# Attention with a threshold and a shrinking layer on one core: some k and q turned on TensorE instead of by DMA, v loaded in three pieces, other slots

## The chip, the cores and the metric

The kernel runs on one core of a Trainium2 chip. The metric is the device time in microseconds (us) of one execution. Inputs lie in HBM as 32-bit floats, and the output goes there too. The engines of the core are TensorE (PE, with its weight loads shown apart as PEld), VectorE (DVE), ScalarE (ACT), GpSimd (POOL) and SyncE (SP), which here only issues DMAs.

## The reference

```python
# q, k, v: (8, 8, 576, 64); tau = 0.02
scores = scale * np.matmul(q, k.transpose(0, 1, 3, 2))       # scale = 1/8
thresh = np.max(scores, axis=-1, keepdims=True) - tau
scores = np.where(scores >= thresh, scores, -1e9)
attn = softmax(scores)
x = np.matmul(attn, v)            # -> (8 * 576, 512): heads side by side
h = x @ w_in                      # w_in (512, 2048)
out = (h - np.tanh(h)) @ w_out    # w_out (2048, 512)
```

## The kernel before, in words

**Pairs and tiles.** The 64 heads are taken two at a time, as 32 pairs (p = 0 to 31, four per batch entry). A pair has 9 tiles of 128 score rows: four for each head, and one that both share, since 576 rows are 4.5 x 128. The shared tile is the last one of an even pair and the first one of an odd pair, so two shared tiles stand next to each other, once in 18 tiles (their matmuls are on L387, all others on L396). There are 288 tiles.

**Work for a pair.** k, q and v are loaded. `split` (L222, GpSimd) scales k or q and writes it as a high and a low 16-bit half side by side (khl, qhl). `turn` (L297) transposes these nine 128x128 blocks into kT or qT of 128x1152. `swap` (L318, GpSimd) writes kS, which is kT with its halves exchanged. `split_v` (L255, GpSimd) writes v into one of four buffers vb.

**Work for a tile.** `scores` (L373): matmuls of qT with kT and kS into a PSUM tile psS of the pool ps_big, which has two buffers; VectorE scales it into sc and takes its row maxima (L406). `kink` (L425): ScalarE makes z from sc with the threshold. z is transposed, by TensorE for the first six pairs (L452), later by a DMA that SP issues for two tiles at once (L440, zT). `weights` (L442): ScalarE's exponential gives pT (L469). `attend` (L474): matmuls with vb into psO. `norm` and `emit_x` bring the result to xT.

**The layer.** Once the four pairs of a batch entry are done, `layers` (L630) hands out 16 h steps (four matmuls, L565, then tanh on ScalarE, L578, and a subtraction on VectorE, L584) and 16 y steps (four matmuls, L591). A string PATTERN (L622) says for each of 36 slots which step comes in it. After the last tile the rest of the layer runs alone.

**The order.** There is no scheduler: every engine executes its instructions in the order in which the main loop (L820) issues them. A slot s issues the scores of tile s + 8, kink of tile s + 5, weights of tile s, the layer steps of the slot, attend, and last the steps in `plan[s]`. The tables PREP (for pairs 1 to 7) and LATER (for pairs from DUAL = 8 on, one for even and one for odd pairs, L746) put a pair's loads, splits, turns and swap into the plan. An entry (what, d) means: d slots ahead of the slot that issues the pair's first scores, which is 9p - 8. k0, q0, q1, v0, v1 are loads, ks, qs, vs the splits, kt, qt the turns, and kw the swap.

**Who turns.** For pairs below 8, `turn` uses nine transposing matmuls (L281) into a PSUM tile of ps_big and one VectorE copy (L313), then calls `swap`. From pair 8 on, both k and q go through a transposing DMA that SP issues (L301), and the swap is a plan step of its own. The same SP queue issues the zT transposes and the stores of the output.

**Loads from pair 8 on** are issued by ScalarE (`load_part`, L143). v goes in two DMAs: four of the nine rows of each group to partitions 0 to 63, five to partitions 64 to 127. The pools of raw data, khl and qhl, and kT, qT and kS have two buffers for each name.

Of the kernel before, what the change touches and what calls it, by code (L numbers as in the profile page):

```python
# [9 lines left out]
F32 = mybir.dt.float32  # L10
# [8 lines left out]
def kernel(  # L19
# [12 lines left out]
    P = 128  # L32

    B, H, S, D = q.shape
# [11 lines left out]
    HPAIR = H // 2  # L46
# [5 lines left out]
    TPP = 9  # L52
# [10 lines left out]
    AHEAD = 8  # L63
# [48 lines left out]
    raw_pool = pool("raw", 2)  # L112
# [21 lines left out]
    raws = {}  # L134
    DUAL = 8
    AT_ONCE = 1
    LOADER = nc.scalar

    boths = {}

    def load_part(p, t, part):  # L143


        b, h0 = p // HPAIR, 2 * (p % HPAIR)
        if part == 0:
            both = raw_pool.tile([P, 2, 10, D], F32, name=f"{t}raw", tag=t)
            both = boths[t] = both[:, 0:AT_ONCE, :, :]
            for a in range(AT_ONCE):  # L150
                raws[p + a, t] = both[:, a, :, :]
        both = boths[t]
        rows = {"k": k, "q": q, "v": v}[t][b, h0 : h0 + 2 * AT_ONCE, :, :]
        heads = both.rearrange("p a (h c) d -> p (a h) (c d)", h=2)
        if t == "k":
            dst = both[:, :, 0:TPP, :].rearrange("p a c d -> p a (c d)")
            rows = rows.rearrange("(a h) s d -> a (h s) d", h=2).rearrange(
                "a (p c) d -> p a (c d)", c=TPP
            )
        elif t == "v":  # L160
            rows = rows.rearrange("h (p c) d -> p h (c d)", c=TPP)
            if part == 0:
                dst, rows = heads[0:64, :, 0 : 4 * D], rows[:, :, 0 : 4 * D]
            else:
                dst, rows = heads[64:P, :, :], rows[:, :, 4 * D :]
        elif part == 0:
            dst = heads[:, :, 0 : 4 * D]
            rows = rows[:, 0:512, :].rearrange("h (p c) d -> p h (c d)", c=4)
        else:
            dst = both[:, part - 1, 4, :]  # L170
            rows = rows[2 * part - 2 : 2 * part, 512:S, :].rearrange("h s d -> s h d")
        LOADER.dma_start(out=dst, in_=rows)

    def load(p, t):
        b, h0 = p // HPAIR, 2 * (p % HPAIR)
        hs = slice(h0, h0 + 2)
        src = {"k": k, "q": q, "v": v}[t]
        eng = nc.sync
        r = raw_pool.tile([P, 2, 10, D], F32, name=f"{t}raw", tag=t)[:, 0, :, :]
        raws[p, t] = r  # L180
        eng.dma_start(
            out=r.rearrange("p (h c) d -> p h (c d)", h=2)[:, :, 0 : 4 * D],
            in_=src[b, hs, 0:512, :].rearrange("h (p c) d -> p h (c d)", c=4),
        )
        rem = src[b, hs, 512:S, :].rearrange("h s d -> s h d")
        if t == "v":
            eng.dma_start(out=r[0:64, 4:10:5, :], in_=rem)
        else:
            eng.dma_start(out=r[:, 4, :], in_=rem)

    def load_first(t, h, eng):

        src = {"k": k, "q": q}[t]
        if (0, t) not in raws:
            raws[0, t] = raw_pool.tile([P, 2, 10, D], F32, name=f"{t}raw", tag=t)[:, 0, :, :]
        r = raws[0, t]
        if h is None:
            rem = src[0, 0:2, 512:S, :].rearrange("h s d -> s h d")
            eng.dma_start(out=r[:, 4, :], in_=rem)
        else:  # L200
            eng.dma_start(
                out=r[:, 5 * h : 5 * h + 4, :].rearrange("p c d -> p (c d)"),
                in_=src[0, h, 0:512, :].rearrange("(p c) d -> p (c d)", c=4),
            )
# [17 lines left out]
    def split(p, t):  # L222
        x = raws.pop((p, t))[:, 0:9, :]
        hl = hl_pool.tile([P, TPP, 2, D], FP16, name=f"{t}hl", tag=t)
        nc.gpsimd.tensor_scalar(  # L225
            out=x, in0=x, scalar1=QKSC, scalar2=1.0, op0=ALU.mult, op1=ALU.mult
        )
        nc.gpsimd.tensor_copy(out=hl[:, :, 0, :], in_=x)
        nc.gpsimd.tensor_tensor(  # L229
            out=hl[:, :, 1, :], in0=x, in1=hl[:, :, 0, :], op=ALU.subtract  # L230
        )
        hls[p, t] = hl
# [22 lines left out]
    def split_v(p):  # L255
        r, vb = raws.pop((p, "v")), vbs[p % NV]
        lo = 64 if p >= DUAL else 0
        nc.gpsimd.tensor_copy(
            out=vb[:, :, 0:4, 0:D],
            in_=r.rearrange("p (h c) d -> p h c d", h=2)[:, :, 0:4, :],  # L260
        )
        nc.gpsimd.tensor_copy(out=vb[0:64, :, 4, 0:D], in_=r[lo : lo + 64, 4:10:5, :])
        nc.gpsimd.tensor_copy(out=vb[64:P, :, 5, 0:D], in_=r[lo : lo + 64, 4:10:5, :])
# [13 lines left out]
    def turn_chunk(out, c, lhsT, mixed=True):  # L277
# [4 lines left out]
            out=out, lhsT=lhsT, rhs=rhs, is_transpose=True, start=True, stop=True  # L282
        )

    def k_lead(p):
        if p < HPAIR + 2:
            return 6 if p in (2, 4) or p == HPAIR + 1 else 5 - (p == 1)
        return (6, 6)[1 - p % 2]

    def q_by_dma(p):  # L290

        return p >= DUAL

    def k_by_dma(p):
        return p >= DUAL

    def turn(p, t):  # L297
        hl = hls.pop((p, t))
# [19 lines left out]
    def swap(p):  # L318
        m = mats[p, "k"]
        sw = qk_tile("ks")  # L320
        for lo, hi in ((0, D), (D, 0)):
            o, i = sw[lo : lo + D, 0:W], m[hi : hi + D, 0:W]
            nc.gpsimd.tensor_copy(out=o, in_=i)  # L323
        mats[p, "ks"] = sw
# [264 lines left out]
    def project(m, ms, part, ps, last, cols=slice(0, d_model)):  # L589
# [31 lines left out]

    PATTERN = lambda m: {  # L622
        0: '-h--h-hh--h-hh-h-hh-h--hh-h--hh-y-yy',
        B - 2: 'hyhyhyhyhyhyhyhyhyhyhyhyhyhyhyhy',
    }.get(m, 'h-yhyhhyhyyhyyhh-yhhyhhy-yhyyh-yyhhy')

    FIRST = 3
    quarters = lambda m: [(m, ms, part) for ms in range(4) for part in range(4)]
# [86 lines left out]
    def w_cast():  # L715
        flat, wt, i, cols = loaded.pop(0)
        nc.gpsimd.tensor_copy(out=flat[:, i * cols : (i + 1) * cols], in_=wt)  # L717

    def w_load(piece):
# [6 lines left out]
        else:  # L726
# [18 lines left out]

    LATER = {  # L746
        0: (
            ("k0", 17), ("q0", 15), ("v0", 13), ("kt", 7), ("q1", 15),
            ("ks", 8), ("v1", 12), ("vs", 6), ("qs", 10), ("qt", 7),
            ("kw", 3),  # L750
        ),
        1: (
            ("k0", 19), ("v1", 14), ("q0", 18), ("v0", 16), ("qs", 11),
            ("q1", 17), ("qt", 8), ("ks", 13), ("vs", 6), ("kt", 10),
            ("kw", 7),
        ),
    }
    for p in range(DUAL, NPAIR):
        first = TPP * p - AHEAD
        at = lambda d, f: plan.setdefault(first - d, []).append(f)  # L760
        for what, d in LATER[p % 2]:
            t, w = what
            f = {
                "0": lambda p=p, t=t: load_part(p, t, 0),
                "1": lambda p=p, t=t: load_part(p, t, 1),
                "2": lambda p=p, t=t: load_part(p, t, 2),
                "s": lambda p=p, t=t: split_v(p) if t == "v" else split(p, t),
                "t": lambda p=p, t=t: turn(p, t),
                "w": lambda p=p, t=t: swap(p) if k_by_dma(p) else None,
            }[w]  # L770
            at(d, f)
    for p in range(1, DUAL):
        first = TPP * p - AHEAD
        for d, f in PREP[3 if p == 1 else 0 :]:
            d -= p == 1 and d == 3
            if p > HPAIR and d >= LDK - 2:
                d = ((16, 14, 12), (17, 15, 13))[1 - p % 2][LDK - d]
            elif d in (7, 8) and q_by_dma(p):
                d = ((9, 9) if d == 7 else (10, 10))[1 - p % 2]
            elif d == 4:  # L780
                d = 4
            elif d == 5:
                d = k_lead(p)
            elif p in (2, 4):
                d = {8: 9, 7: 8}.get(d, d)
            plan.setdefault(first - d, []).append(lambda p=p, f=f: f(p))
        d = (6, 7)[1 - p % 2] if q_by_dma(p) else 3 - (p == 1 or p >= 5)
        d = 4 if p in (2, 4) else d
        plan.setdefault(first - d, []).append(lambda p=p: turn(p, "q"))

    load(0, "v")
# [8 lines left out]
        load(1, t)  # L800
    pieces = w_pieces()
    load_when = [3, 8, 13, 18, 21, 25, 29, 34, 38, 42, 46, 49, 52, 55, 58, 61]
    cast_when = [11, 19, 27] + [4 * i + 32 for i in range(3)] + [3 * i + 44 for i in range(10)]

    todo, stage = [], 0
    fold = const.tile([P, 64], BF16, name="fold")
# [3 lines left out]
            plan.setdefault(-AHEAD, []).extend(plan.pop(at))  # L810


    kinks, wts, atts = {}, {}, {}
    for i in range(NTILE + 3):
        at = i - 4 if i < HPAIR * TPP else i
        atts.setdefault(at + LAG, []).append(i)
        if i < NTILE:
            wts.setdefault(at, []).append(i)
            kinks.setdefault(i // 2 * 2 + 2 - AHEAD if i < 4 else i - MASK, []).append(i)
    for s in range(-AHEAD, NTILE + LAG + 3):  # L820
        p, j = divmod(max(s, 0), TPP)
# [43 lines left out]
                emit_x(pp - 1)  # L865
        for step in plan.pop(s, []):
            step()
        if s + AHEAD in cast_when:
            w_cast()
        if s + AHEAD in load_when:  # L870
            w_load(next(pieces))

    for _, step in todo:
# [16 lines left out]
    _ = bass_utils  # L890
# [35 lines left out]
```

## Time and profile before

| what | value |
|---|---|
| three timed runs | 511.3, 513.72, 514.99 us; median 513.72 |
| the profiled execution | 509.47 us, of which the span of the trace is 507.7 |
| TensorE's mean granted clock | 0.995 |
| DMA | 95.61 MB, 234,525 packets, 205,152 of them under 512 B |
| SP's DMA queue | 213,520 packets, 73.17 MB, 74.7% of 16 engines |
| ScalarE's DMA queue | 20,944 packets, 21.67 MB, 15.7% of 16 engines |
| transposing DMAs | zT x117, kT x24, qT x24; median 4.4 to 4.9 us from issue to landing |
| transposing matmul on k or q | 72 each, a record of 220 ns |
| copy of its PSUM tile on VectorE | 757 ns |

The page of the profile first gives each engine's busy time, share of the span and number of instructions; then the span in 40 equal slices, where a digit is the busy share in tenths; then the DMA queues, the chain of work that ended last, and the costliest groups of instructions. In an answer by windows each engine's busy time stands with its number of instructions, and the granted clock, the DMA share and GB/s close the line. A DMA share above 1 comes from packets that overlap. In a timeline a row has start, duration, engine, line, operation and tiles, and in brackets the idle time ahead of it with what ended it. The ends of matmuls are modelled, so their starts are the surer numbers.

### The profile page before, as it was taken

To read this page: it belongs to the slowest core of one execution; us is meant where nothing else is said; L and a number is where in the kernel's file an instruction comes from. 1 tells how busy PE (TensorE), PEld (TensorE's weight loads), DVE (VectorE), ACT (ScalarE), POOL (GpSimd) and SP (SyncE) were. 2 spreads that over 40 slices of the span, in tenths; PEclk is the share of its full clock that TensorE was granted. 3 is DMA by queue.
4 is the path that set the end of the run, shared out by engine and by line. 5 is a ranking of instruction groups with operands and counts; after the bars stand their busy time and mean duration, and the time that the engine had idled before them with its cause. 6 is when DMAs were issued, how large, how long until landed. Compare 5 with 4: busy or idle time off the path is not lost.

```text
span 507.7 us, 12146 instructions
## 1 busy us (share of the span) xinstructions
PE 484.1 (95%) x4274; PEld 270.4 (53%) x4336; DVE 400.0 (79%) x1149; ACT 432.7 (85%) x617; POOL 291.1 (57%) x390
## 2 busy tenths in 40 slices
PE   8999899888999999999999999999998999999997
PEld 4667566444555555555555555555554555544444
DVE  5899979976989898988898889889887887544440
ACT  5999999988999999999999999999998999533430
POOL 7999999967676657574757575575567500000000
PEclk9999999998999999999999999999999999999999
DMA  6852658999999999999999999999999976211013
GB/s 198 264 163 90 196 176 220 226 189 220 211 245 228 242 227 223 242 249 211 228 228 268 216 228 228 223 231 231 212 220 252 197 131 113 76 41 43 24 40 83
DMA packets 234525, 95.61 MB, mean 188 GB/s; under 512 B 205152, under 2 KB 223840, under 8 KB 234464
## 3 DMA queue, kind: packets, MB, share of 16 engines
q1 hardware_dynamic: 213520, 73.17, 74.7%
q10 hardware_dynamic: 20944, 21.67, 15.7%
q8 instruction: 34, 0.56, 0.5%
q14 instruction: 27, 0.22, 0.1%
HBM read 36.70 MB, written 9.44 MB: 91 GB/s over the span
## 4 chain that ended last, share of the span: by engine, by line
PE 61%; POOL 12%; DMA 10%; ACT 6%; issue 5%; DVE 3%; ACTq 1%; SPq 0%; POOLq 0%
PE psY L591 20%; PE psH L565 16%; PE psS L396 14%; PE psO L499 4%; DMA zT<-z 3%; POOL kS L323 3%; PE psHt L565 3%; ACT pT L469 3%; ACT z L433 2%; DMA kT<-khl 2%; DMA kraw<-in_k_dram 2%; PE psS L387 2%; ACT th L578 1%; POOL w_in_sb L717 1%; DMA qraw<-in_q_dram 1%
## 5 line engine op out<-in xcount | busy, mean ns | idle before, releaser
L406 DVE TENSOR_SCALAR_CACHE_REDUCE sc<-psS 128x576 f32<-128x576 f32 x288 | 213.2, 752 | 28.7 <-PE psS L396 14.2
L433 ACT ACTIVATE z<-sc,nb 128x576 bf16<-128x576 f32 x288 | 217.2, 770 | 13.5 <-DVE nb L418 9.4
L591 PE MATMUL psY<-w_out_sb,g 128*128 128x512 bf16 (+1 forms) x564 | 141.5, 375 | 1.7 <-DVE nb L418 0.2
L469 ACT ACTIVATE pT<-zT 128x1152 f16<-128x1152 bf16 x117 | 135.0, 1154 | 4.6 <-DMA zT<-z 4.6
L565 PE MATMUL psH<-xT,w_in_sb 128*128 128x512 bf16 x448 | 118.8, 379 | 5.3 <-DVE g L584 2.2
L323 POOL COPY kS<-kT 64x1152 f16<-64x1152 f16 x62 | 70.7, 1141 | 74.6 <-DMA kT<-khl 55.2
L584 DVE SCALAR_TENSOR_TENSOR g<-th,psH 128x512 bf16<-128x512 f32 x128 | 87.6, 684 | 28.9 <-ACT th L578 28.1
L396 PE MATMUL psS<-kT,qT 128*128 128x512 f16 (+1 forms) x512 | 104.8, 286 | 3.3 <-DVE sc L406 1.5
L396 PE MATMUL psS<-kS,qT 128*128 128x512 f16 (+1 forms) x512 | 104.9, 287 | 0.1
L396 PEld LDWEIGHTS <-qT 128*128 128x128 f16 x1024 | 72.8, 98 | 58.6 <-issue 4.2
L578 ACT ACTIVATE th<-psH 128x512 f32<-128x512 f32 x128 | 74.6, 583 | 20.9 <-PE psH L565 20.9
L591 PEld LDWEIGHTS <-g 128*128 128x128 bf16 x592 | 51.3, 98 | 55.1 <-issue 1.1
L565 PEld LDWEIGHTS <-w_in_sb 128*128 128x128 bf16 x576 | 49.0, 98 | 57.3 <-issue 5.5
L499 PE MATMUL psO<-vb,pT 128*128 128x65 bf16 x1024 | 53.6, 195 | 0.0
L499 PEld LDWEIGHTS <-pT 128*128 128x128 f16 x1024 | 44.5, 98 | 9.9
L229 POOL TENSOR_TENSOR qhl<-qraw,qhl 128x576 f16<-128x576 f32 x31 | 39.7, 1281 | 2.6
L229 POOL TENSOR_TENSOR khl<-kraw,khl 128x576 f16<-128x576 f32 x31 | 39.7, 1280 | 2.6
L461 ACT ACTIVATE pT<-psZ 128x512 f16<-128x512 bf16 (+1 forms) x54 | 35.1, 653 | 2.5 <-PE psZ L452 2.3
L225 POOL TENSOR_SCALAR qraw<-qraw 128x576 f32<-128x576 f32 x31 | 20.8, 670 | 20.9 <-DMA qraw<-in_q_dram 19.6
L603 DVE COPY yo<-psY 128x512 f32<-128x512 f32 (+1 forms) x31 | 21.1, 680 | 13.3 <-PE psY L591 12.4
L492 PE MATMUL psO<-vb,pT 128*128 128x130 bf16 x128 | 28.3, 221 | 2.1 <-ACT pT L469 1.8
L525 DVE TENSOR_TENSOR osb<-psO,rc 128x256 bf16<-128x256 f32 x64 | 27.2, 425 | 2.2
(77 smaller groups left out, 448.6 us busy)
## 6 DMA issues: line engine op xcount, KB each, us to landing
out_dram<-yo SPq DMA_DIRECT2D x32, 256.0 KB, 2.9
kraw<-in_k_dram ACTq DMA_DIRECT2D x24, 288.0 KB, 4.2
qraw<-in_q_dram ACTq DMA_DIRECT2D x24, 256.0 KB, 4.1
wt<-in_moe_w_in_dram SPq DMA_DIRECT2D x8, 512.0 KB, 4.6
wt<-in_moe_w_out_dram SPq DMA_DIRECT2D x8, 512.0 KB, 4.2
vraw<-in_v_dram ACTq DMA_DIRECT2D x24, 160.0 KB, 4.0
vraw<-in_v_dram ACTq DMA_DIRECT2D x24, 128.0 KB, 4.2
vraw<-in_v_dram SPq DMA_DIRECT2D x8, 256.0 KB, 3.6
```

Source lines behind the costliest of these rows:

```text
L229: nc.gpsimd.tensor_tensor(out=hl[:, :, 1, :], in0=x, in1=hl[:, :, 0, :], op=ALU.subtract)
L323: nc.gpsimd.tensor_copy(out=o, in_=i)
L396: nc.tensor.matmul(out=ps[:, dst], lhsT=lhs, rhs=cols(p, kk, hh), start=(n == 0), stop=(n == 1),)
L406: nc.vector.tensor_scalar(out=sc, in0=ps[:, lo : lo + S], scalar1=SC, scalar2=None, op0=ALU.mult, op1=ALU.max, accum_out=mx[:, c : c + 1],)
L433: nc.scalar.activation(out=z, in_=sc, func=ACT.Prelu, bias=nb, scale=1.0, alpha=STEEP)
L461: nc.scalar.activation(out=pt[:, off * P : (off + n) * P], in_=ps[:, 0 : n * P], func=ACT.Exp)
L469: nc.scalar.activation(out=pt[:, 0 : n * P], in_=zts.pop(i)[:, 0:n, :], func=ACT.Exp)
L499: nc.tensor.matmul(out=po[:, t - 1 + ab, :], lhsT=pt[:, blk * P : (blk + 1) * P], rhs=vb[:, hh, c, :], start=False, stop=(n == 7), skip_gr ...
L565: nc.tensor.matmul(out=ps, lhsT=w_in_sb[:, c, n * P : (n + 1) * P], rhs=xs[m][:, c, :] if m < B else xR[:, c, :, :], start=(c == 0), stop= ...
L578: nc.scalar.activation(out=th, in_=ps, func=ACT.Tanh)
L584: nc.vector.scalar_tensor_tensor(out=gs[m][:, n, :], in0=th, scalar=-1.0, in1=ps, op0=ALU.mult, op1=ALU.add,)
L591: nc.tensor.matmul(out=ps, lhsT=gs[m][:, n, ms * P : (ms + 1) * P], rhs=w_out_sb[:, n, cols], start=(n == 0), stop=(n == DF_C - 1),)
```

## The change

The turn of k for pairs 8, 12, 16, 20, 24 and 28 (every fourth from the ninth on) and for pair 9, and the turn of q for pair 8, use the matmuls that pairs below 8 use. For these k the swap follows inside `turn`, and the plan step kw does nothing. v's second DMA (five rows) becomes two (four rows and one). The tables LATER get a third entry, "pe", for pairs 12, 16, 20, 24 and 28, and FIRST_LATER holds pairs 8 and 9. Most other entries move by a slot or a few. The turn of k of pair 5 moves from slot 6 to slot 5 ahead; the other LEADS are what the code gave before. PATTERN is another string for stage 1 and for stages 2 to 5. The raw tiles are allocated at half their size, of which half was unused. The lists cast_when and SOONER are written otherwise, with the same values.

```diff
+    V_PARTS = ((0, 0, 4), (64, 4, 8), (64, 8, 9))
...
-            if part == 0:
-                dst, rows = heads[0:64, :, 0 : 4 * D], rows[:, :, 0 : 4 * D]
-            else:
-                dst, rows = heads[64:P, :, :], rows[:, :, 4 * D :]
+            at, c0, c1 = V_PARTS[part]
+            dst = heads[at : at + 64, :, c0 % 4 * D : (c1 - c0 + c0 % 4) * D]
+            if c0 == 8:
+                dst = heads[at : at + 64, :, 4 * D : 5 * D]
+            rows = rows[:, :, c0 * D : c1 * D]
...
     def q_by_dma(p):
-        return p >= DUAL
+        return p >= DUAL and p != 8
     def k_by_dma(p):
-        return p >= DUAL
+        return p >= DUAL and p % 4 != 0 and p != 9
...
+        1: 'h-yhhyhyhyhyyyhh-yhhyhhy-yyhyh-yyhhy',
         B - 2: 'hyhyhyhyhyhyhyhyhyhyhyhyhyhyhyhy',
-    }.get(m, 'h-yhyhhyhyyhyyhh-yhhyhhy-yhyyh-yyhhy')
+    }.get(m, 'y-hhyyhyhhyhyyh-hyhhyhhyhyy-yhyy-hhy')
...
     LATER = {
         0: (
-            ("k0", 17), ("q0", 15), ("v0", 13), ("kt", 7), ("q1", 15),
-            ("ks", 8), ("v1", 12), ("vs", 6), ("qs", 10), ("qt", 7),
-            ("kw", 3),
+            ("k0", 17), ("q0", 15), ("v0", 13), ("kt", 8), ("q1", 15),
+            ("ks", 10), ("v1", 12), ("v2", 10), ("vs", 6), ("qs", 13),
+            ("qt", 7), ("kw", 2),
         ),
         1: (
-            ("k0", 19), ("v1", 14), ("q0", 18), ("v0", 16), ("qs", 11),
-            ("q1", 17), ("qt", 8), ("ks", 13), ("vs", 6), ("kt", 10),
-            ("kw", 7),
+            ("k0", 18), ("v1", 14), ("v2", 12), ("q0", 18), ("v0", 16),
+            ("qs", 10), ("q1", 17), ("qt", 9), ("ks", 13), ("vs", 5),
+            ("kt", 11), ("kw", 7),
+        ),
+        "pe": (
+            ("k0", 17), ("q0", 16), ("v0", 13), ("kt", 7), ("q1", 14),
+            ("ks", 8), ("v1", 13), ("v2", 12), ("vs", 6), ("qs", 9),
+            ("qt", 8), ("kw", 3),
+        ),
+    }
+    FIRST_LATER = {
+        8: (
+            ("k0", 18), ("q0", 15), ("v0", 14), ("kt", 7), ("q1", 15),
+            ("ks", 8), ("v1", 12), ("v2", 11), ("vs", 6), ("qs", 8),
+            ("qt", 5), ("kw", 3),
+        ),
+        9: (
+            ("k0", 19), ("v1", 15), ("v2", 13), ("q0", 18), ("v0", 16),
+            ("qs", 11), ("q1", 17), ("qt", 8), ("ks", 10), ("vs", 6),
+            ("kt", 6), ("kw", 5),
         ),
     }
...
-        for what, d in LATER[p % 2]:
+        for what, d in FIRST_LATER.get(p) or LATER[p % 2 if k_by_dma(p) else "pe"]:
```

## The prediction

> **What bounds the kernel now.** I read the page from the busy shares to the slices, then the waits, then the order of time itself. TensorE is busiest; the 40 slices say where it is not.
>
> ```profile
> PE 484.1 (95%) x4274; PEld 270.4 (53%) x4336; DVE 400.0 (79%) x1149; ACT 432.7 (85%) x617; POOL 291.1 (57%) x390
> ...
> PE   8999899888999999999999999999998999999997
> ...
> DMA  6852658999999999999999999999999976211013
> ```
>
> A modelled 95% proves little, so I measure it with landmarks. The scores of the two shared tiles (L387) come once in 18 tiles; the timeline gives their starts: 87.55, 113.95, 144.35, 169.93, 197.23, 222.81, 250.11, 275.69, 302.99, 328.57, 356.94, 382.52, 412.53. From 144.35 on the distances repeat: 25.58 and 27.30 us. The pattern strings put 15 and 17 layer steps (h or y) into them, so a step is (27.30 - 25.58) / 2 = 0.86 us, which is what four 128x512 matmuls take in the chain, and everything else 25.58 - 15 x 0.86 = 12.68 us. A stretch that is exactly its matmuls is bound by TensorE. Against this rule: 113.95 to 144.35 holds 16 steps, 26.44 us, and took 30.40: 3.96 lost. 328.57 to 356.94 lost 28.37 - 27.30 = 1.07. 382.52 to 412.53 holds 18 steps, 28.16, and took 30.01: 1.85 lost. Together 6.88 us. From 87.55 to 113.95 only 10 steps fall (21.3 us of TensorE work in 26.40): there ScalarE, not TensorE, sets the pace.
>
> The answer by windows shows the hole and a regular stretch (columns: length; PE, PEld, DVE, ACT, POOL busy; clock; DMA share; GB/s):
>
> ```profile
> 100.00:120.00 20.00, 15.37 (x135) 8.46 (x136) 15.20 (x47) 17.43 (x25) 14.71 (x19) 0.93 1.20 214
> ...
> 200.00:220.00 20.00, 19.84 (x176) 11.13 (x178) 18.29 (x55) 19.60 (x28) 11.72 (x16) 1.00 1.22 243
> ```
>
> In the regular one TensorE idles 0.16 us and ScalarE 0.4, and the DMA share is as high as in the hole: three resources near their limit. What opened the hole, in the timelines of SP's queue, GpSimd and TensorE:
>
> ```profile
> 106.37 3.30 SPq L301 DMA_TRANSPOSE qT<-qhl  x1
> 109.77 12.07 SPq L440 DMA_TRANSPOSE zT<-z  x5
> ```
> ```profile
> 109.99 2.33 POOL L323 COPY kS<-kT 64x1152 f16<-64x1152 f16 x2 [4.34 <-DMA kT<-khl]
> ```
> ```profile
> 117.39 0.29 PE L492 MATMUL psO<-vb,pT 128*128 128x130 bf16 x1 [1.81 <-ACT pT L469]
> ...
> 119.30 1.49 PE L591 MATMUL psY<-w_out_sb,g 128*128 128x512 bf16 x3 [0.22 <-DVE nb L418]
> ```
>
> A q transpose holds SP 3.30 us where the median is 1.44, five zT behind it take 2.4 each instead of 1.3 to 1.5, and the chain has a zT landing after 5.31 us at 115.08. The exponentials wait for it, TensorE for them (1.81), and afterwards it runs slowly: three matmuls in 1.49 us instead of 0.65. The two later losses begin the same way, with a zT of 6.96 us at 324.27 and a q load of 6.59 at 374.98.
>
> **What the Trainium skill says.** "TensorE: Matmul & The Clock Gate", section "Part 1: The HAM clock gate", has the array fall to half clock after about 3.4 us of too little work and return after as long: the granted 0.93 and the 1.49 agree, so a wait of 1.81 costs twice that. The same page, "Part 4: PE-mode transpose", says that such a transpose ends in PSUM and needs a VectorE copy, and gives about 275 ns in a kernel; here a record is 220 ns, but nine in a row advance the queue by 80.57 - 80.06 = 0.51 us, and I use that. "DMA: Bandwidth & Descriptors", "Issuing engines are not separate DMA queues": SP's and ScalarE's transfers share the same 16 engines. The trace agrees: a late transpose and a late load in the same jams. Its section "Why small descriptors are slow (HBM only)" charges a fixed cost per packet; the queue of ScalarE's loads shows 15.7% of 16 x 507.7 us for 20,944 packets, 61 ns each.
>
> **The change part by part.**
>
> *Eight transposes leave SP and the DMA engines* (k of 8, 9, 12, 16, 20, 24, 28; q of 8). SP: 8 x 1.42 us of issue. Engines: SP's queue spent 74.7% of the span on 213,520 packets, 28 ns each; a transpose moves 294,912 B, by estimate 1,152 packets of 256 B, so 1,152 x 28 / 16 = 2.0 us. Eight save 16 us of DMA time, three of them just ahead of and in the hole.
>
> *72 transposes on TensorE.* 8 x 0.51. Those of pairs 8 and 9 fall into slots 57, 59 and 67, in the stretch where TensorE has about 5 us to spare: free under ScalarE's work; 1.5 us without that cover. The other five lie in stretches that are exactly TensorE's: 5 x 0.51 = **2.55 us**, paid in full.
>
> *Eight VectorE copies* of 0.757. VectorE is busy 17.7 of 20 us, so each backlog is gone in about 7 us; behind it stand the row maxima, used by ScalarE three slots (4.4 us) later. Taken as 0; uncovered 5 x 0.76 = 3.8. The turn also takes one of two score buffers, back after about 1.3 us, when the next score needs it two slots on: 0.
>
> *Swaps.* For these k they move from GpSimd's slot 3 to 7, right behind the turn, and wait for the VectorE copy. Behind them stand split_v and the next pair's k split. For pair 12: k is split by 146.97 in the old trace, the turn comes near 148.5, the swap runs about 150 to 152.4 (old: 153.83 to 156.2), the next k split ends near 156.6, and SP could issue that kT (old: 157.72) no earlier, as its buffer is read until about then. 0, if the turn is not late.
>
> *A new wait.* TensorE's turn now waits for GpSimd's split; all matmuls stand behind it. In the old trace the splits of pairs 12, 16, 20, 24, 28 end at 146.97, 198.95, 252.27, 304.22, 358.77; the turn's slot (landmark plus two slots and steps) ends near 148.5, 201.4, 254.3, 307.3, 361.1: 1.5 to 3 us of margin. The second q load, which stands ahead of that split, is a slot (1.5 us) later, the large one a slot earlier. Taken as 0; the price is in the third case.
>
> *v in three.* 24 more ScalarE issues. In the timeline the next activation starts on its usual distance (th 0.67 after z, with an issue between): 0 when nothing blocks. The extra piece has 128 packets of 256 B: at most 24 x 128 x 61 / 16 = 12 us of DMA time, at least 0 if the shorter main piece gives it back; I take 6, leaving a net relief of 10 us.
>
> *Other slots.* k of odd pairs turns a slot earlier, which can hold SP for one slot until the old buffer is read; the next zT on that queue comes two slots later: 0. q and k splits move by up to 3 slots; they run when data is there. Pair 5's k a slot later, 36 layer slots reordered, 32 steps a stage as before: 0, with 1 us either way. Weight loads and casts unchanged.
>
> *What the relief returns.* The 3.96 us, since all three early turns leave the queue that was late; and half of the other 2.92, as the five later ones come once in four pairs: 5.42 of 6.88, 79%. Sum on the profiled execution: 509.47 (span 507.7 and 1.8 around it) - 5.42 + 2.55 = 506.6. But it is faster than all three timed runs (511.3 to 515.0, median 513.72). Its matmuls can't differ from theirs, so I book the 4.25 to the median as more of the same late transfers: 11.1 us of loss there, 79% is 8.8: 513.72 - 8.8 + 2.55 = **507.5 us**.
>
> **The rivals.** *Hidden or eaten relief.* The high DMA share in regular stretches at no loss says that engine time alone isn't what hurts; jams come from coincidence, new slots make new ones, and the extra packets (up to 12 of 16 us) eat the saving. Then a third returns: 513.72 - 3.7 + 2.55 = 512.6. Against it: the first jam names k and q transposes. *The turn becomes the wait, and the kernel slower.* Loads of 5.6 to 6.6 us occur; if q's second load lands 1.5 to 3 us later than now, split and turn are late and TensorE stops with everything behind it. A stop of 1.8 us cost 3.96; five such are 19.8: 513.72 - 8.8 + 2.55 + 19.8 = 527.3. It decides from about 2.9 us a turn (14.6 in all, against 6.2 gained and 1% of the time) on. Against it: the margins, and that the large q load leaves earlier. That the change doesn't happen is excluded: the order of instructions has 72 more matmuls with 72 weight loads and eight transposes fewer.
>
> **How the numbers follow.** Relief works: 0.64, from 503 (all 11.1 returned and the 2.55 half hidden: 503.9, 1 us for order) to 511; of this 0.56 below 508.6 and 0.08 above. Eaten: 0.23, from 510 to 517, nearly all within 1%. Late turns: 0.13, 518 to 530. About 1%, 5 us, is what a measurement can tell from no change. So faster 0.56, same 0.31, slower 0.13; the range 503 to 518.5 leaves out about 0.15. The likeliest case alone: 503 to 511.
>
> **What would show it.** Right: between the landmarks near 114 and 144 about 26.4 us, clock 1.00 from 100 to 140, no psO wait of 1.8; nine-fold turns of 0.5 us on TensorE with the five stretches 0.5 longer; SP's transposes at 1.3 to 1.5 us. Wrong: TensorE idle at a turn "<-POOL khl", clock dips near 148, 201, 254, 307, 361; or the old holes kept, with zT waits and longer v landings.

## The result, and the profile after

The changed kernel takes 515.82 us in the median of 20 runs, the kernel before 514.17 in 20 runs beside it: a ratio of 1.0032, 95% interval 1.0007 to 1.0056. That is no change by the bound of 1%; 507.5, a gain of 1.2%, was forecast. All ratios leave out executions more than 1.5% above the fastest of the same kernel (one of the changed kernel's 20, at 618.32 us), while the medians given hold all of them. The profiled execution took 515.64 us with a span of 513.9. It is a typical one. The profiled execution of before (509.47) was not: none of the 20 runs beside it is below 510.52. So the two spans exaggerate the difference, and ratios of many runs decide below. The medians of the kernel before differ from one group of runs to the next (514 to 518), so every ratio is to runs of the kernel before in the same group, on the same chip. The changed kernel was timed again in a later group, at 0.9979; between groups, differences of up to about half a per cent therefore prove little.

The busy shares and the slices of after:

```profile
PE 492.5 (96%) x4408; PEld 274.7 (53%) x4408; DVE 406.2 (79%) x1157; ACT 432.8 (84%) x617; POOL 292.2 (57%) x390
...
PE   8999899979999999999899999999999999999997
...
DMA  7852659999999999999999999999999985411013
```

In the answer by windows, the stretch that held the hole, and a later one (length; PE, PEld, DVE, ACT, POOL busy; clock; DMA share; GB/s):

```profile
100.00:120.00 20.00, 16.60 (x158) 9.03 (x158) 16.67 (x50) 18.74 (x25) 15.48 (x20) 1.00 0.91 172
...
240.00:260.00 20.00, 18.61 (x166) 10.08 (x165) 15.37 (x46) 17.83 (x25) 11.54 (x15) 1.00 1.18 229
```

The clock no longer falls (0.93 before) and the DMA share is 0.91 instead of 1.20, as fits three transposes fewer. TensorE still idles 3.4 us in it, and a later stretch has a hole of 1.4 us that was not there.

The landmarks (first L401 row of each double shared tile, which was L387) say it stretch by stretch. Each stretch is held against 12.68 us plus 0.86 for each layer step:

| stretch | steps | without loss, no turn | before | after |
|---|---|---|---|---|
| pair 8/9's own (from 88) | 10 | ScalarE's pace | 26.40 | 28.66 |
| the next one | 16 | 26.44 | 30.40 | 27.03 |
| with a turn on TensorE (five) | 15 | 25.58 | 25.58 each | 26.87, 26.88, 26.19, 26.19, 26.68 |
| between these (four) | 17 | 27.30 | 27.30, 27.30, 27.30, 28.37 | 27.68, 30.24, 27.95, 28.10 |
| the last | 18 | 28.16 | 30.01 | 28.43 |

The two old holes shrink by 3.37 and 1.58. The first stretch loses 2.26, the turn stretches 4.9 in all, and the 17-step ones 3.7. What TensorE waits for in after names the new places (columns: us in total, times, longest):

```profile
PE psX L556 <- DVE g L598: 2.7, 4, 1.3
PE psS L410 <- DVE sc L420: 2.5, 7, 0.6
PE psH L579 <- DVE g L598: 1.9, 5, 0.9
...
PE psS L410 <- DVE kT L327: 1.2, 1, 1.2
PE psS L410 <- DMA qT<-qhl: 1.0, 1, 1.0
```

In this order they were 1.1, 1.5, 2.2, 0.4 and nothing before. The last one is a jam of the old kind at a new place, in the stretch of 30.24: a q transpose held SP for 2.65 us at 232.33, and the scores waited for it:

```profile
232.33 2.65 SPq L315 DMA_TRANSPOSE qT<-qhl  x1
```
```profile
239.81 0.42 PE L410 MATMUL psS<-kT,qT 128*128 128x512 f16 x2 [0.96 <-DMA qT<-qhl]
```

The DMA queues of after:

```profile
q1 hardware_dynamic: 204048, 70.81, 72.9%
q10 hardware_dynamic: 24400, 21.67, 16.6%
```

SP's queue (q1) has 9,472 packets fewer but only 0.747 x 507.7 - 0.729 x 513.9 = 4.6 us less engine time, and ScalarE's (q10) has 3,456 packets and 5.6 us more. That looked like the answer, v's pieces eating the relief, and was the first theory to test. (Such differences of two traces turned out to be uncertain by some 10 us; see the last section.)

### The profile page after: what moved, and what is told of

Same layout as the page of the kernel before. It is cut to its first block, busy times and chain, and to the rows that moved or that the text cites. A ratio compares the mean times of both kernels' runs of the same rounds, so it can differ in the third digit from the quotient of the medians.

```text
span 513.9 us, 12360 instructions
## 1 busy us (share of the span) xinstructions
PE 492.5 (96%) x4408; PEld 274.7 (53%) x4408; DVE 406.2 (79%) x1157; ACT 432.8 (84%) x617; POOL 292.2 (57%) x390
## 3 DMA queue, kind: packets, MB, share of 16 engines
q1 hardware_dynamic: 204048, 70.81, 72.9%
q10 hardware_dynamic: 24400, 21.67, 16.6%
## 4 chain that ended last, share of the span: by engine, by line
PE 32%; DMA 21%; POOL 17%; ACT 14%; issue 6%; DVE 5%; ACTq 3%; SPq 0%; POOLq 0%; DVEq 0%
PE psY L605 12%; DMA zT<-z 9%; PE psH L579 8%; DMA qraw<-in_q_dram 6%; ACT z L447 5%; ACT pT L483 5%; PE psS L410 5%; ACTq L175 3%; ACT th L592 3%; POOL qhl L232 3%; PE psHt L579 3%; DMA kraw<-in_k_dram 2%; POOL kS L337 2%; POOL khl L232 2%; DMA kT<-khl 2%
## 5 line engine op out<-in xcount | busy, mean ns | idle before, releaser
L605 PE MATMUL psY<-w_out_sb,g 128*128 128x512 bf16 (+1 forms) x592 | 145.7, 373 | 0.0
L483 ACT ACTIVATE pT<-zT 128x1152 f16<-128x1152 bf16 x117 | 135.0, 1154 | 11.5 <-DMA zT<-z 11.4
L579 PE MATMUL psH<-xT,w_in_sb 128*128 128x512 bf16 x480 | 123.3, 379 | 2.1 <-DVE g L598 1.9
L410 PEld LDWEIGHTS <-qT 128*128 128x128 f16 x1024 | 73.9, 97 | 63.0 <-issue 6.9
```

Source lines behind the costliest of these rows:

```text
L410: nc.tensor.matmul(out=ps[:, dst], lhsT=lhs, rhs=cols(p, kk, hh), start=(n == 0), stop=(n == 1),)
L483: nc.scalar.activation(out=pt[:, 0 : n * P], in_=zts.pop(i)[:, 0:n, :], func=ACT.Exp)
L579: nc.tensor.matmul(out=ps, lhsT=w_in_sb[:, c, n * P : (n + 1) * P], rhs=xs[m][:, c, :] if m < B else xR[:, c, :, :], start=(c == 0), stop= ...
L605: nc.tensor.matmul(out=ps, lhsT=gs[m][:, n, ms * P : (ms + 1) * P], rhs=w_out_sb[:, n, cols], start=(n == 0), stop=(n == DF_C - 1),)
```

## The experiments

Every kernel was timed beside the kernel before. Results are ratios to it, with the 95% interval.

**1. Parts alone, and parts undone.** Theory V is v's third piece, T the price of the turns, S the moved slots and patterns.

```diff
 # a_two_v, on the changed kernel (and no "v2" in the tables)
-    V_PARTS = ((0, 0, 4), (64, 4, 8), (64, 8, 9))
+    V_PARTS = ((0, 0, 4), (64, 4, 9))
 # a_dma_turns, on the changed kernel
-        return p >= DUAL and p % 4 != 0 and p != 9
+        return p >= DUAL                     # and q likewise; same tables
 # b_pe_turns, on the kernel before
-        return p >= DUAL
+        return p >= DUAL and p % 4 != 0 and p != 9    # q: p != 8
 # b_three_v, on the kernel before (and ("v2", 10) or ("v2", 12) in the tables)
+            at, c0, c1 = ((0, 0, 4), (64, 4, 8), (64, 8, 9))[part]
```

> The changed kernel with v again in two DMAs, all else as changed. Before is 514.2 us, the changed kernel 515.8. Theory V (the extra 3,456 packets of v eat the DMA relief: ScalarE's queue rose by 5.6 us of engine time while SP's fell by 4.7): the relief comes back, about 511 us, and the share of ScalarE's queue falls from 16.6% to 15.7%. Theory T (the turns' 5 x 0.5 us on TensorE are the cost, and the relief is worth little anyway): 515 to 516. Theory S (the moved slots make the transposes late): 515 to 516.

> The changed kernel with all turns of pairs from 8 on by DMA again, slots, pattern and v as changed. Theory T: it loses the turns' price and no more, 513 us. Theory V: eight transposes more on top of the extra packets, 519 us or more. Theory S: the late transposes stay and get somewhat worse, 517 to 520.

> The kernel before with only the eight turns moved to TensorE, slots, pattern and v as before. Theory T: 514.2 + 2.5 = 516.7 us, up to 518 if the three early turns are not hidden. Theories V and S: without the extra packets or the new slots the relief shows, 509 to 512 us, and the stretch of 30.4 us between the landmarks at 114 and 144 falls to about 26.4.

> The kernel before with only v in three DMAs (the third one two slots after the second), turns, slots and pattern as before. Theory V: it costs about the 5.6 us of engine time, 517 to 520 us. Theories T and S: 513.5 to 515, the pieces are hidden.

Measured: a_two_v 0.9999 (0.9974 to 1.0025), a_dma_turns 1.0098 (1.0067 to 1.0128), **b_pe_turns 0.9909 (0.9883 to 0.9936)**, b_three_v 0.9985 (0.9953 to 1.0017).

The turns alone make the kernel faster by 0.9%, and the changed kernel without them is 1% slower than before. A part of that last figure is owed to its slots, which are set for turns on TensorE: TensorE waits 5.1 us for kS in its trace and 0.4 in the changed kernel's. So the relief is real, and everything else in the change costs about what it brings. V falls: the third piece by itself costs nothing that these runs can tell, and with two pieces the share of ScalarE's queue was 17.1%, not the lower one that V expected. T falls. S stands, but is several things. In the trace of b_pe_turns the stretch after the landmark at 114.5 takes 27.31 us, not 30.40, and TensorE is busy through the old hole:

```profile
100.00:120.00 20.00, 18.23 (x174) 10.14 (x174) 17.25 (x52) 19.40 (x27) 16.11 (x21) 1.00 1.08 196
```

**2. What the rest consists of.** Three parts were added to the turns, one at a time, and the pattern was taken from the changed kernel.

```diff
 # t_pattern: b_pe_turns and
+        1: 'h-yhhyhyhyhyyyhh-yhhyhhy-yyhyh-yyhhy',
-    }.get(m, 'h-yhyhhyhyyhyyhh-yhhyhhy-yhyyh-yyhhy')
+    }.get(m, 'y-hhyyhyhhyhyyh-hyhhyhhyhyy-yhyy-hhy')
 # t_first: b_pe_turns and the changed slots of pairs 8 and 9 (no "v2")
 # t_rest: b_pe_turns and the changed slots of pairs 10 to 31 (no "v2")
 # a_old_pattern: the changed kernel, with the opposite of t_pattern's edit
```

> The kernel before with the eight turns on TensorE (0.991 of before by itself) and also the two new pattern strings; slots and v as before. Theory P (the new order of layer steps costs what the turns gain): 1.002 to 1.006 of before. Theory L (the moved slots of loads, splits and turns cost it): 0.989 to 0.993.

> The kernel before with the eight turns on TensorE and also the new slots of pairs 8 and 9 alone; the other slots, the pattern and v as before. Theory L1 (the slots of the first two pairs cost, since TensorE waited 1.2 us for VectorE's copy of k and that stretch took 28.7 us in the changed kernel against 26.9 with the turns alone): 0.994 to 0.997 of before. Theory P: 0.989 to 0.993.

> The kernel before with the eight turns on TensorE and also the new slots of pairs 10 to 31; the slots of pairs 8 and 9, the pattern and v as before. Theory L2 (these slots cost, by transposes and splits that come at worse moments): 0.996 to 1.003 of before. Theories P and L1: 0.989 to 0.993.

> The changed kernel (1.003 of before) with the old pattern strings. Theory P: most of the turns' gain appears, 0.991 to 0.995 of before. Theory L: 1.001 to 1.005.

Measured: t_pattern 0.9976 (0.9944 to 1.0008), t_first 0.9945 (0.9916 to 0.9973), t_rest 0.9961 (0.9929 to 0.9993), a_old_pattern 0.9956 (0.9927 to 0.9985).

By the ratios the pattern costs 0.7% on top of the turns, and taking it out of the changed kernel gives back 0.8%. But both set ratios of different groups against each other. Against the second ratio of the changed kernel, 0.9979, the pattern gives back only 0.2%, with overlapping intervals. So the pattern costs something between 0.2 and 0.8% by these kernels. The slots of pairs 8 and 9 cost 0.4% by the ratio, within the intervals, but the landmarks are clearer: their stretch takes 29.00 us in t_first and 26.18 in t_rest. For pairs 10 to 31 the ratio says 0.5% and the trace nothing: the 17-step stretches of t_rest take 27.30, 27.30, 27.37 and 27.30, its span of 506.1 is the shortest of all, and its median of 511.67 us is the lowest of the four kernels here (the others 513.38 to 514.39). What these slots cost, if anything, stays open.

**3. Is it the DMA load?** On t_rest, each of the eight turns also issues the transposing DMA that it replaced. The copy goes to a spare tile that nothing reads; the raw tiles have half their size here, as in the changed kernel.

```diff
+        if p >= DUAL:
+            spare = qk_pool.tile([P, W], FP16, name="spare", tag="spare")
+            nc.sync.dma_start_transpose(
+                out=spare[:, 0:W].rearrange("p (c r) -> p c r", c=TPP),
+                in_=hl.rearrange("p c a d -> p (c a d)"),
+            )
```

> The kernel before with the eight turns on TensorE and the new slots of pairs 10 to 31 (0.996 of before, the lowest median of its group), and for each of the eight turns also the transposing DMA that it replaced, into a spare tile that nothing reads: the DMA load of before with the TensorE load of the change. Theory R (the gain of the turns is the relief of SP's queue and the DMA engines): the gain is gone and the turns' 2.5 to 4 us stay, 1.003 to 1.010 of before. Theory K (the gain comes from k being ready sooner on TensorE, not from the DMA load): no more than 0.2% above the kernel without the spare DMAs.

Measured: 1.0016 (0.9989 to 1.0043). The gain is gone: the ratio is 0.55% above t_rest's and a little below what theory R expected. The two stand in different groups and their intervals just overlap; the medians say it more clearly: t_rest lies 1.2% below the kernel before of its group, this one 0.1% above. About half of the old hole is back as well: the stretch after the landmark at 115.31 takes 28.95 us, against 27.29 in t_rest and 30.40 before. The same window in t_rest, then with the spare transposes:

```profile
100.00:120.00 20.00, 18.46 (x178) 10.55 (x180) 17.63 (x56) 19.89 (x28) 16.56 (x22) 1.00 0.97 188
```
```profile
100.00:120.00 20.00, 17.23 (x160) 9.44 (x160) 16.77 (x51) 18.68 (x26) 15.09 (x18) 1.00 1.19 218
```

Both programs have the same matmuls. With a DMA share of 1.19 instead of 0.97, TensorE and ScalarE each get 1.2 us less done in this window. The waits of pT for zT rise from 3.2 to 8.2 us over the span, a weaker sign, since b_pe_turns shows 12.3. The relief is therefore that of the removed transposing DMAs, as the prediction said. This run does not part SP's issue time from the load of the 16 engines, as the spare transposes bring back both; they also hold the tiles they read.

**4. Mending the changed kernel.**

```diff
 # a_psx
-    }.get(m, 'y-hhyyhyhhyhyyh-hyhhyhhyhyy-yhyy-hhy')
+    }.get(m, 'y-hhyyhyhyhhyyh-hyhhyhhyhyy-yhyy-hhy')
 # a_first_old: FIRST_LATER holds the slots of before (with "v2")
 # a_mended: both
```

> The changed kernel with one h and one y exchanged in the string of stages 2 to 5 (positions 9 and 10), so that no two h steps stand right ahead of emit_x, whose PSUM tile is of the same two-buffer pool. Theory X (the new pattern costs by this wait of psX for g, 2.7 us in four stages, and what follows it): it loses 2 to 3 us against the changed kernel, 0.997 to 1.000 of before, and no psX wait over 0.3 us is left in these stages. Rival (the pattern costs otherwise): no change from 1.003.

> The changed kernel with the old slots of pairs 8 and 9 (v's third piece two slots after the second). Theory L1 (these slots cost 1.2 to 2.2 us between the landmarks near 88 and 116): that stretch falls from 28.7 to 27 us or less, and the time to 0.998 to 1.001 of before. Rival (the jam only moves to the next stretch): the sum of the two stretches stays at 55.7, time 1.003.

> The changed kernel with both, the exchanged steps and the old slots of pairs 8 and 9. Theories X and L1 together: 0.991 to 0.996 of before, near the turns alone. If the three pieces of v or the other slots matter as well: 0.997 to 1.003.

Measured: a_psx 1.0001 (0.9975 to 1.0027), a_first_old 0.9988 (0.9960 to 1.0017), a_mended 0.9990 (0.9967 to 1.0013).

The slots of 8 and 9 behave as L1 said: in a_first_old their stretch takes 26.47 us with the old ones. Over all kernels with the turns it takes 28.05 to 29.35 with the new slots (eight of them) and 26.18 to 27.57 with the old (six, leaving out the one with spare transposes, 27.87). That is 1.9 us by the means. The next stretch gives back 0.5, and the one ahead takes 0.3 more, so these slots cost about 1.7 us. The exchange of two steps is a miss, and so is a_mended, for which 0.991 to 0.996 was expected. The psX waits of stages 3 to 5 go, but psH, from the same two-buffer pool, waits in their place (longest 0.9 us), since the exchange only put the pair of h steps right behind emit_x:

```profile
PE psH L579 <- DVE g L598: 5.0, 9, 0.9
```

**5. Which half of the string.** The two halves were put back separately, with the changed kernel beside them on one chip.

```diff
 # a_old_prefix
+    }.get(m, 'h-yhyhhyhyyhyyh-hyhhyhhyhyy-yhyy-hhy')
 # a_old_tail
+    }.get(m, 'y-hhyyhyhhyhyyhh-yhhyhhy-yhyyh-yyhhy')
 # t_three_v: b_pe_turns with b_three_v's edit;  a_again: the changed kernel
```

> The changed kernel with the first 15 characters of the string of stages 2 to 5 as before, the last 21 as changed; stage 1 as changed. Theory X (the two h steps ahead of emit_x in the new first half cost): most of the pattern's 0.76% returns, 0.4 to 0.7% below the changed kernel of the same call, and the 17-step stretches fall from 27.7 to 30.2 us to 27.3 to 27.6. Rival (the tail costs): 0 to 0.2%.

> The changed kernel with the last 21 characters of that string as before and the first 15 as changed. Theory X: 0 to 0.2% below the changed kernel of the same call, psX waits for g of 0.5 to 1.3 us still there in stages 3 to 5. Rival (the tail costs): 0.4 to 0.7% below.

> The kernel before with the eight turns on TensorE and v in three DMAs; slots and pattern as before. Theory V2 (the extra packets take back a third of the turns' gain): 0.993 to 0.996 of before. Rival (the pieces are free): 0.989 to 0.992, as the turns alone.

> The changed kernel, for comparison with the other three on one chip: 1.000 to 1.006 of before by what was measured; if the first measurement's chip was a special one, down to 0.997.

Measured: **a_old_prefix 0.9893 (0.9844 to 0.9942, six runs)**, a_old_tail 0.9992 (0.9960 to 1.0024), **t_three_v 0.9845 (0.9793 to 0.9896, six runs)**, a_again 0.9979 (0.9951 to 1.0007).

The first half of the string costs 0.86% by the two ratios, the tail nothing. By the medians of the same runs it is less, 513.63 us against 515.51 for a_again, or 0.4%, and the spans of the two traces, 510.7 and 511.9, are only 1.2 us apart. The direction is the same in all three; the size is not settled. The 17-step stretches show where it is lost: 27.96, 28.58, 27.90, 28.20 in a_again, 28.00, 27.92, 28.22, 27.80 with the old tail, and 27.30, 27.31, 27.30, 27.30 with the old first half. TensorE, and then ScalarE and VectorE, in stage 3 of a_again show why:

```profile
242.38 1.03 PE L579 MATMUL psH<-xT,w_in_sb 128*128 128x512 bf16 x4
243.74 1.03 PE L579 MATMUL psH<-xT,w_in_sb 128*128 128x512 bf16 x4
...
246.47 0.38 PE L556 MATMUL psX<-ident_bf,osb 128*128 128x128 bf16 x4 [1.11 <-DVE g L598]
```
```profile
245.12 0.58 ACT L592 ACTIVATE th<-psH 128x512 f32<-128x512 f32 x1
...
245.73 0.69 DVE L598 SCALAR_TENSOR_TENSOR g<-th,psH 128x512 bf16<-128x512 f32 x1
```

Counted from 0, the new string has h steps at positions 8 and 9, and `emit_x` in slot 9 wants a tile of the pool that these two have just filled. The first comes free only when its tanh, which ScalarE reaches at 245.12 behind z and pT, and its subtraction are done, at 246.42. With the old first half position 9 is a y step, and no such wait is left in a_old_prefix. That the waits (2.8 us in a_again) make up most of what the stretches lost (0.66 + 1.28 + 0.60 + 0.90 = 3.4 us) ties this loss to them. Not all of it is net: the five stretches with a turn take 134.4 us in a_old_prefix and 132.7 in a_again, so 1.7 us were lost again there. And a_old_pattern, which has the old first half too and no wait of psX, still shows two 17-step stretches of 27.83 and 27.91 us.

t_three_v confirms that v in three costs nothing with the turns either. It is the best ratio measured, and its two old holes have shrunk to 27.36 and 28.35 us (30.40 and 30.01 before). Its interval overlaps that of the turns alone, so whether the pieces help is not shown. The sum of the good parts, the changed kernel with the old pattern and the old slots of pairs 8 and 9, was not measured. Stage 1's string and the turn of pair 5 were not changed alone either.

## Why the prediction was wrong, point by point

The forecast was 507.5 us and 515.8 came, 8.3 more. Single traces find most of it: about 2.4 us in the price of the turns, 1.7 in the slots of pairs 8 and 9, 2.7 in waits of psX, and 1.0 in one late q transpose.

**Right: what bounded the kernel, and that relief returns.** The turns alone gave 0.9909, which is 4.7 us of 514 (3.3 to 6.0 by the interval). Their price on TensorE (below) was about 4.6, so about 9.3 us of loss returned; 8.8 had been booked. That the two lie so close is partly luck, since 4.25 of the 11.1 us of loss were read from no trace, and the price is that of another kernel, t_rest. The spare transposes took the gain back. The old hole of 30.40 us shrank to 26.55 to 28.24 in every kernel with the turns and without those transposes; 26.44 would be without loss.

**Right: a stop costs about twice its wait.** By windows of 2 us the clock granted to TensorE in the kernel before was 0.85, 0.50 and 0.80 from 116 to 122. That is 1.7 us of lost clock, or 3.4 us at half rate, and with the wait of 1.81 it makes 3.5 of the 3.96 us lost. TensorE had not been idle for long before: it was busy for 1.9 of the 4 us from 114 to 118.

**Wrong: the step "other slots", which had the 36 reordered steps, the moved splits and loads at 0, with 1 us either way.** This is the step that failed. By the runs the pattern costs between 0.2 and 0.9% (1 to 4.4 us), of which the traces with the new first half show 2.1 to 3.6 us as waits of psX (1.1 before), and the slots of pairs 8 and 9 about 1.7 us. The waits that could be named are for a buffer of a pool of two. For the pattern I counted the steps of a stage and not who takes the two buffers of ps_h next to emit_x. For pair 9 the forecast that the turn's hold on one of two score buffers costs 0 failed. With the turn in its new slot, the second score after it waits for the VectorE copy of k to give the buffer back. The copy stands behind two row maxima, a g and two copies, of which the last three are shown:

```profile
109.82 0.69 DVE L598 SCALAR_TENSOR_TENSOR g<-th,psH 128x512 bf16<-128x512 f32 x1
110.42 0.41 DVE L569 COPY xT<-psX 128x512 bf16<-128x512 bf16 x1
110.76 0.21 DVE L570 CAST xR<-psX 128x64 bf16<-128x64 f32 x1
110.89 0.74 DVE L327 COPY kT<-ps_k 128x1152 f16<-128x1152 f16 x1
```
```profile
109.29 0.67 PE L284 MATMUL ps_k<-ident_f,khl 128*128 128x128 f16 x9
...
111.69 0.41 PE L410 MATMUL psS<-kT,qT 128*128 128x512 f16 x2 [1.20 <-DVE kT L327]
```

With the old slots the longest such wait is 0.4 us, so this explains less than half of the 1.9 us; where the rest of that stretch went is open.

**Under-sized: the turn, 2.55 us for five.** Nine transposes do advance the queue by 0.51, but the stretches with a turn grew by more: 27.17, 26.51, 26.26, 26.26, 26.26 in t_rest, where 25.58 is the floor. That is 0.9 each and 4.6 in all, and 4.9 in the changed kernel. The part of it that the trace names is TensorE waiting for a score buffer behind the turn, since only one of the two is free: 0.85 us at 147.15 in t_rest, and 0.27 here:

```profile
200.02 0.67 PE L281 MATMUL ps_k<-ident_f,khl 128*128 128x128 f16 x9
200.96 0.41 PE L396 MATMUL psS<-kT,qT 128*128 128x512 f16 x2 [0.27 <-DVE sc L406]
```

The one that gives the buffer back here is the row maxima of the score before (sc), not the copy of k, and in these five stretches of t_rest no wait for a copy is listed. So it is again the 0 for the score buffer that failed, not the 0 for the copies.

**Half right: three turns free in ScalarE's stretch.** In t_rest and t_three_v, with the old slots, that stretch takes 26.18 us against 26.40 before, so the turns are free there. In the four other kernels with the old slots it takes 26.47 to 27.57, and in the new slots the turns are not free.

**Right in effect, open in size: DMA time.** 16 us off SP's queue were forecast. Between the two main traces it is 4.6, between t_rest and the kernel with spare transposes 16.8 (last section). v's extra packets, counted as 3,072 and in fact 3,456, were put at 0 to 12 us with 6 taken; 5.6 came between the two main traces, but no loss in the kernel's time followed.

**Right: no late turn.** No turn from pair 8 on shows a wait for GpSimd's split in the changed kernel, so the slower rival did not come. (Its threshold was mis-added: 6.2 us gained and 1% of the time are about 11.4, or 2.3 a turn, not 14.6 and 2.9.) The time came nearest to the "eaten relief" rival, for half of its reasons: the packets ate nothing that could be measured, but the new slots did make a jam, the late q transpose of 1.0 us. The larger part went to two-buffer pools, which that rival did not name.

**Two misread lines.** I took 12.07 us for five zT on SP's queue as a sign of the jam. t_rest has the same run of five in 12.94 us, and its stretch of 27.29 us lost 0.85 where 3.96 were lost before: such a row also spans SP's waits, 8.6 us of them for z here. And the three matmuls in 1.49 us should be held against 0.81, which a row of three takes elsewhere, not against 0.65.

```profile
107.17 12.94 SPq L440 DMA_TRANSPOSE zT<-z  x5
```

## What to carry to other kernels

When a change moves work and also reorders its neighbours, cost the reordering by buffers and not by counts alone: for each pool of two buffers write down who takes a tile in each slot, and which engine's queue gives it back. The price of work on the bounding engine is its issue time plus what the next user of its output buffer waits for. And when one profiled execution is faster than every timed run, sum against it, but take ratios of many runs for the verdict.

## What the runs showed of the hardware that was not expected

The time that a queue's packets take is no steady price. Fourteen kernels have the same 204,048 packets on SP's queue, and their engine time (share times span) runs from 366.7 to 376.2 us. In the four with 213,520 packets it is 378.4, 379.3, 383.2 and 389.3. So the 9,472 packets of eight transposes are worth 4.6 us between the kernels before and after, and 16.8 between t_rest and the kernel with the spare transposes:

```profile
q1 hardware_dynamic: 204048, 70.81, 73.6%
```
```profile
q1 hardware_dynamic: 213520, 73.17, 75.8%
```

At the mean of 28 ns for each packet 16.6 us were to be expected. One pair of traces can neither confirm nor refute such a sum. ScalarE's queue scatters likewise: 79.7 to 87.7 us with 20,944 packets and 84.0 to 91.9 with 24,400. The 24 more loads behind these, with 3,456 more packets, left the kernel's time where it was (0.9985, 0.9953 to 1.0017).
